# Attention and SwiGLU on one core: q and k columns dealt by groups of four heads, and all first-phase weights on one queue

## The chip, the cores and the metric

The kernel runs on one core of a Trainium2 chip. Such a core has a matrix engine (TensorE, PE in the profile, with PEld for its weight loads), a vector engine (DVE), a scalar engine (ACT), a general engine (POOL) and a synchronisation engine (SP) that here does nothing but issue DMAs. The metric is device time in microseconds; lower is better. Three runs of the kernel before took 590.81, 593.8 and 593.9 us, median 593.8.

## The reference

One token sequence x (2048 x 576, bf16) is normalised, and the result feeds two branches whose outputs are added to x.

```python
xn = layernorm(x)                                     # over 576, eps 1e-5
q, k, v = (xn @ wqkv) split into 32 heads of 18       # D = 576
scores = q @ k^T * 18**-0.5, causal, window 256
A = softmax(scores) @ v @ wo
B = (silu(xn @ w1) * (xn @ w3)) @ w2                  # F = 4608
out = x + A + B
```

## The kernel before

The sequence is worked off in four chunks of 512 tokens. Each chunk has three stages, one after the other on PE: QKV (about 13.6 us), the first phase (36 units of the first MLP product, w1 and w3, with the attention of the chunk dealt in between, 85 to 91 us), and the second phase (the product with w2 and the output product with wo, 42 to 46 us). Chunk 0 begins with the load and layernorm of the tokens instead of a ready xnT. The layernorm of chunk c+1 runs within the first phase of chunk c, on DVE, POOL and PE (`ln_stats`, `ln_apply`, `xn_turn`).

A unit u computes 128 of the 4608 hidden columns: 9 pairs of matmuls (line 646), each pair on the two halves of PE's rows, one into the bank of "up" and one into that of "gate"; then a tanh on ACT (654) and two operations on DVE (660, 663) that write hT. Its weights come in sets: `load_w13` fetches 512 columns of w3 and of w1 as two halves of 576 KB, enough for four units (`w13_at` names the buffer; there are three, and the fourth set of the run goes into a part of hT that is not needed yet). A set is released after unit 4m+3 and needed at unit 4m+12, so nine sets per chunk are on their way two or three ahead. Half w3 is issued by SP, half w1 by ACT, where `load_w13((), "act")` stands; in the first sets of the run SP issues both. One set per chunk is loaded in two halves during the second phase of the chunk before, at items 70 and 170 of its list.

The heads are 18 wide and so do not line up with 128 rows. QKV's matmuls for q and k give tiles of 128 columns, as the columns stand in wqkv: tiles 0 to 3 are q columns 0 to 511, 4 to 7 k columns 0 to 511, tile 8 the last 64 columns of both. They are evacuated into `stage`, one half of a pair by DVE, the other by ACT. From there `repack` moves every group of four heads by DMA into `qv` and `kv`, the layouts that the score matmuls want: a group needs 6 to 8 DMAs, more where it crosses a tile's border. `Groups` says which groups are complete after which tile. In chunks 1 to 3, groups 0 to 2 are issued during QKV, the other five at units 0, 1, 4, 7 and 8 (line 502 for all). `kv` has twelve blocks of keys: eight of the chunk, and the last four of the chunk before, which POOL copies (`keep_keys`).

Attention runs in steps: a score step is a few matmuls (541), an exponential on ACT into a slot (550: ten slots in `pt`, four in hT's tail, four in `stage` once it is free), masks on POOL (577). When two groups are done, `pv` multiplies with v, and after a normalisation DMAs pack the result into oT (631).

The order is written out in the program, engine by engine, by `add`; each engine works in that order, and an instruction that waits holds up all behind it. `_Prog.resolve` puts semaphore waits where data or buffers ask for them. Each of SP and ACT has a DMA queue of its own. On SP stand x tiles (296), w13 (316), w2 (333), the xnS swap (378), repack (502), oT (631) and the output (711). A counter of PE work (`clock`) decides between which matmul pairs of the units a score step is put.

## Time and profile before

The profiled execution took 591.38 us, 589.7 of it the span that the profile covers.

| stage | from to, us | length | PE busy | clock granted | GB/s |
|---|---|---|---|---|---|
| start and QKV, chunk 0 | 0 to 22.6 | 22.6 | 19.14 | 1.00 | 235 |
| first phase, chunk 0 | 22.6 to 109.3 | 86.7 | 82.64 | 0.98 | 175 |
| second phase, chunk 0 | 109.3 to 152.9 | 43.6 | 42.20 | 1.00 | 186 |
| QKV, chunk 1 | 152.9 to 166.5 | 13.6 | 13.60 | 1.00 | 55 |
| first phase, chunk 1 | 166.5 to 257.3 | 90.8 | 86.20 | 0.98 | 132 |
| second phase, chunk 1 | 257.3 to 301.7 | 44.4 | 42.17 | 1.00 | 169 |
| QKV, chunk 2 | 301.7 to 315.3 | 13.6 | 13.60 | 1.00 | 54 |
| first phase, chunk 2 | 315.3 to 400.9 | 85.6 | 84.09 | 1.00 | 140 |
| second phase, chunk 2 | 400.9 to 446.5 | 45.6 | 42.42 | 1.00 | 162 |
| QKV, chunk 3 | 446.5 to 460.0 | 13.5 | 13.50 | 1.00 | 55 |
| first phase, chunk 3 | 460.0 to 545.2 | 85.2 | 83.21 | 1.00 | 108 |
| second phase, chunk 3, to the end | 545.2 to 589.7 | 44.5 | 41.73 | 1.00 | 111 |

PE is the busiest engine at 96% of the span; DVE has 54%, ACT 43%, POOL 27%. The table is read row against row: the same work is done in the second phase of every chunk, and in the first phase of chunks 1 to 3 (but the last chunk has no next layernorm), so that differences between rows of one kind are waits or a slower clock. In the rows of the profile that follow, a group is line, engine, operation, output and inputs, shape and count; after the bar busy time and mean duration in ns, after the second bar the engine's idle time before these instructions and what ended it. A row of the timeline is start, length, what ran and how often, and in brackets the idle time before it. SPq and ACTq are the DMA issues of SP and ACT. "Issue" as a releaser means that the profile shows no wait that ended.

### The profile page before, as it was taken

Reading aid. Unit: us, or ns where it says so; the run is one execution under the profiler, and the core shown is the slowest. Engines: PE = TensorE matmul, PEld = TensorE weight load, DVE = VectorE, ACT = ScalarE, POOL = GpSimd, SP = SyncE. Lnnn points to the kernel's source line nnn. Section 1 sums busy time; section 2 is a strip of 40 time slices with the busy share of each in tenths; the row PEclk is TensorE's granted clock in tenths of the full one; section 3 lists DMA queues with packets and bytes.
Section 4 is the critical chain, followed back from the end, with each engine's and each line's share of the span. In section 5 each row is a group of like instructions: output and inputs, shape, how many; then the busy total and the mean of one; then the engine's idle time right before and its main releaser. Section 6 shows DMA issues by size and latency. Waiting matters only on the chain.

```text
span 589.7 us, 16005 instructions
## 1 busy us (share of the span) xinstructions
PE 564.5 (96%) x6885; PEld 359.9 (61%) x6885; DVE 316.2 (54%) x595; ACT 254.9 (43%) x350; POOL 161.4 (27%) x377
## 2 busy tenths in 40 slices
PE   7998999999999999899999999999899989999998
PEld 4443445677686454467768655457676875554776
DVE  6484887610377768651026777884103566777311
ACT  4354666300176667430017576771002766666000
POOL 6231443400032434240003244443000234434000
PEclk9998999999999999899999999999999999999999
DMA  8999689987317795767741768886773177851452
GB/s 248 179 178 182 129 165 224 204 197 186 95 26 145 123 203 111 155 134 192 173 107 29 138 121 176 148 182 150 166 179 80 39 135 145 159 100 51 114 153 67
DMA packets 119126, 83.87 MB, mean 142 GB/s; under 512 B 25552, under 2 KB 117904, under 8 KB 119056
## 3 DMA queue, kind: packets, MB, share of 16 engines
q1 hardware_dynamic: 98593, 63.41, 50.8%
q10 hardware_dynamic: 20463, 19.44, 16.5%
q8 instruction: 54, 0.88, 0.7%
q14 instruction: 16, 0.13, 0.1%
HBM read 71.29 MB, written 2.36 MB: 125 GB/s over the span
## 4 chain that ended last, share of the span: by engine, by line
PE 72%; DMA 13%; SPq 7%; issue 2%; DVE 2%; ACTq 2%; ACT 1%; POOL 0%
PE ps L646 39%; PE ps L696 14%; DMA w<-in_B_w_dram 9%; PE ps L410 8%; SPq L502 6%; PE ps L541 5%; PE ps L702 3%; PE ps L598 3%; ACTq L631 2%; DMA oT<-od 2%; DMA qv<-stage 1%; ACT xnT L372 0%; DMA xp<-in_A_x_dram 0%; PE ps L365 0%; DVE hT L663 0%
## 5 line engine op out<-in xcount | busy, mean ns | idle before, releaser
L646 PE MATMUL ps<-xnT,w 64*128 64x512 bf16 x1400 | 189.8, 378 | 5.3 <-issue 2.1
L646 PE MATMUL ps<-xnS,w 64*128 64x512 bf16 x1120 | 158.6, 377 | 2.0 <-issue 2.0
L696 PE MATMUL ps<-w,hT 128*128 128x288 bf16 x1152 | 148.6, 286 | 5.6 <-DMA w<-in_B_w_dram 5.4
L550 ACT ACTIVATE pt<-ps 128x1024 bf16<-128x1024 f32 (+1 forms) x112 | 113.2, 1010 | 75.2 <-PE ps L541 75.0
L660 DVE SCALAR_TENSOR_TENSOR gs<-th,ps 128x512 bf16<-128x512 bf16 x144 | 98.0, 680 | 84.9 <-ACT th L654 84.3
L696 PEld LDWEIGHTS ps<-w,hT 128*128 128x128 bf16 x1152 | 111.4, 98 | 38.1 <-DMA w<-in_B_w_dram 7.9
L646 PEld LDWEIGHTS ps<-xnT,w 64*128 64x128 bf16 x1400 | 78.6, 94 | 56.9 <-issue 6.3
L577 POOL TENSOR_TENSOR pt<-pt,mk 128x128 int32<-128x128 int32 (+1 forms) x199 | 80.1, 425 | 87.5 <-ACT pt L550 87.4
L663 DVE SCALAR_TENSOR_TENSOR hT<-gs,ps 128x512 bf16<-128x512 bf16 x144 | 98.9, 687 | 4.9
L654 ACT ACTIVATE th<-ps 128x512 bf16<-128x512 f32 x144 | 85.5, 593 | 27.2 <-PE ps L646 25.5
L646 PEld LDWEIGHTS ps<-xnS,w 64*128 64x128 bf16 x1120 | 65.0, 94 | 51.1 <-issue 2.9
L709 DVE TENSOR_TENSOR ofin<-ps,xp 128x288 bf16<-128x288 f32 x32 | 14.7, 458 | 128.5 <-PE ps L702 128.5
L422 ACT ACTIVATE stage<-ps 128x512 bf16<-128x512 f32 x16 | 9.6, 597 | 154.7 <-PE ps L410 149.5
L541 PE MATMUL ps<-qv,kv 64*128 64x320 bf16 (+2 forms) x720 | 64.4, 253 | 2.0 <-DMA qv<-stage 1.2
L541 PEld LDWEIGHTS ps<-qv,kv 64*128 64x128 bf16 x720 | 41.0, 94 | 32.7 <-issue 2.9
L577 POOL TENSOR_TENSOR hT<-hT,mk 128x128 int32<-128x128 int32 (+1 forms) x31 | 12.4, 422 | 171.4 <-ACT hT L550 171.4
L410 PE MATMUL ps<-xnT,wa 64*128 64x512 bf16 x288 | 34.3, 376 | 0.0
L550 ACT ACTIVATE stage<-ps 128x1024 bf16<-128x1024 f32 x24 | 24.6, 1024 | 13.7 <-PE ps L541 13.4
L620 DVE STREAM_TRANSPOSE od<-oq 128x256 bf16<-128x256 bf16 x64 | 25.8, 427 | 6.3 <-POOL oq L613 6.3
L702 PE MATMUL ps<-wo,oT 128*128 128x288 bf16 x160 | 24.8, 286 | 1.2 <-DMA oT<-od 1.2
L613 POOL TENSOR_TENSOR oq<-uq,rden 128x288 bf16<-128x288 f32 x16 | 10.8, 674 | 54.4 <-DVE rden L612 54.4
L410 PEld LDWEIGHTS ps<-xnT,wa 64*128 64x128 bf16 x288 | 16.7, 94 | 12.4 <-issue 0.7
(59 smaller groups left out, 337.0 us busy)
## 6 DMA issues: line engine op xcount, KB each, us to landing
w<-in_B_w_dram SPq DMA_DIRECT2D x41, 576.0 KB, 7.7
w<-in_B_w_dram SPq DMA_DIRECT2D x72, 288.0 KB, 3.6
w<-in_B_w_dram ACTq DMA_DIRECT2D x29, 576.0 KB, 7.1
xp<-in_A_x_dram SPq DMA_DIRECT2D x29, 144.0 KB, 8.3
out_dram<-ofin SPq DMA_DIRECT2D x32, 72.0 KB, 1.9
kv<-stage SPq DMA_DIRECT2D x105, 18.0 KB
oT<-od SPq DMA_DIRECT2D x84, 18.0 KB
qv<-stage SPq DMA_DIRECT2D x39, 36.0 KB
```

The costliest lines, as they stand in the source:

```text
L410: op = add("pe", lambda e, out_=out_, st=st, mv=mv, n=n, r0=r0, first=first: e.matmul(out_, st, mv, start=first, stop=(part == 1 and n == ...
L502: by, lambda e: e.dma_start(dst, src), r=reads, dma=f"{key[0]}_{g}", **kw)
L541: add("pe", lambda e, r0=r0, out_=out_, kb=kb, q0=q0, nb=nb: e.matmul(out_, kv[r0:r0 + 64, g, kb + NV - NB, :], qv[r0:r0 + 64, g, q0 * KB: ...
L550: add("act", lambda e: e.activation(pt_slot(sl)[:, 0:w, :], PS[:, SC[0]:SC[1] + 1, 0:w].rearrange("p r q -> p q r"), ACT.Exp, scale=scale) ...
L577: add("pool", lambda e, vb=vb, mm=mm: e.tensor_tensor(vb, vb, mm, ALU.mult), r=(key if n == 0 else []) + ["mk"], **{"w" if n == 0 else "j" ...
L620: add("dve", lambda e: e.transpose(od[i][:, c0:c0 + CH // 2], oq[:, c0:c0 + CH // 2]), r=["oq", "oq0"], **{"j" if half else "w": [("od", i)]})
L646: add("pe", lambda e, n=n, r0=r0, r=r, k=k, src=src: e.matmul(PS[:, b0 + r, :], wt[r0:r0 + 64, k, fl * 128:(fl + 1) * 128], src, start=(n ...
L654: add("act", lambda e: e.activation(th[i][:], PS[:, bg, :], ACT.Tanh, scale=0.5), r=[("ps", bg)], w=[("th", i)])
L660: add("dve", lambda e: e.scalar_tensor_tensor(out=gs[i][:], in0=th[i][:], scalar=1.0, in1=PS[:, bg, :], op0=ALU.add, op1=ALU.mult), r=[("t ...
L663: add("dve", lambda e: e.scalar_tensor_tensor(out=hT[:, u, :], in0=gs[i][:], scalar=0.5, in1=PS[:, bu, :], op0=ALU.mult, op1=ALU.mult), r= ...
L696: add("pe", lambda e: e.matmul(bank, hT[:, f, tt * 128:(tt + 1) * 128], w2[sl][:, k, :], start=(f == 0), stop=False), r=[("h", f), ("w2", ...
L702: add("pe", lambda e: e.matmul(bank, oT[:, k, tt * 128:(tt + 1) * 128], wo[:, k, d0:d0 + HD], start=False, stop=(k == 4)), r=[("oT", g) fo ...
```

## The change

There are five parts. In chunks 1 to 3 the columns of q and k are dealt anew: a tile t (0 to 7) holds the q columns of the four heads of group t (72), then the k columns of its first three heads (54), and two columns of the last head's k; tile 8 holds the k columns of the fourth head of groups 0 to 6, and two more of the last head. POOL builds these weights once, in chunk 0, with four copies into `wp`. Chunk 0 still uses the columns as they stand, now from a part of `pt`.

Since every group lies in one tile and in tile 8, one DMA can move the same rows of several groups: `repack_span` is called for group 0, for groups 1 and 2, and for groups 3 to 7 when all tiles are there. It replaces `repack` in chunks 1 to 3; units 0, 1, 4, 7 and 8 issue none any more. The slots in `stage` are all free from the start of the first phase.

All halves of w13 are issued by SP, none by ACT. The set that was loaded in the second phase is loaded in the QKV of the next chunk, behind the repack of groups 1 and 2. In chunk 0 the repack of group 0 comes ahead of set 1 and the two x tiles in SP's order, with its q DMAs on ACT; set 2 follows the repack of group 1. The keys of the chunk before move from the front of `kv` into a tensor of their own, `kb4`.

```diff
+        wv = sb("wv", [128, 5, D])
+        wp = sb("wp", [128, 5, 9, 128])
...
+        kv = sb("kv", [128, G, NB, 2 * KB])
+        kb4 = sb("kb4", [128, G, NV - NB, 2 * KB])
...
+        wa = pt[:, 0:6, :, :].rearrange("p n q r -> p (n q r)")[:, 0:10 * D].rearrange("p (k c) -> p k c", c=2 * D)
+        w8 = pt[:, 6, :, :].rearrange("p q r -> p (q r)")[:, 0:640].rearrange("p (k c) -> p k c", c=128)
+        wa_keys = ["wqk"] + [("pt", n) for n in range(6)]
...
+        def pair_of(c, i):
+            return (i, 4 + i) if c == 0 else ((8, 0), (1, 2), (3, 4), (5, 6))[i]
...
-        PROJ = [("q", 0), ("q", 1), ("v", 0), ("q", 2), ("v", 1), ("q", 3), ("v", 2), ("8", 8), ("v", 3)]
+        PROJ = [("q", 0), ("q", 1), ("v", 0), ("q", 2), ("v", 1), ("q", 3), ("v", 2), ("8", 7), ("v", 3)]
...
+        def keys_of(a, b, p0, n, p):
+            return kv[p0:p0 + n, a:b, :, KB * p:KB * p + KB].rearrange("q g b f -> q (g b) f")
+
+        def repack_span(a, b, eng, q_eng=None):
+            moves = []
+            gs_ = list(range(a, b))
+            for pr in range(2):
+                moves.append(("q", gs_, gs_, qv[64 * pr:64 * pr + 2 * Dh, a:b, :], stage[2 * Dh * pr:2 * Dh * (pr + 1), a:b, :]))
+            for i in range(3):
+                r0 = 4 * Dh + i * Dh
+                moves.append(("k", gs_, gs_, keys_of(a, b, 64 * (i // 2) + Dh * (i % 2), Dh, i % 2), stage[r0:r0 + Dh, a:b, :].rearrange("q g (b f) -> q (g b) f", f=KB)))
+            p0 = 64 + Dh
+            for g in gs_:
+                if g < G - 1:
+                    moves.append(("k", [g], [8], keys_of(g, g + 1, p0, Dh, 1),
+                                  stage[g * Dh:(g + 1) * Dh, 8, :].rearrange("q (b f) -> q b f", f=KB)))
+                else:
+                    for r in range(2):
+                        moves.append(("k", [g], range(9), kv[p0 + r:p0 + r + 2 * 9 - 1:2, g, :, KB:2 * KB], stage[126 + r:127 + r, :, :]))
+            seen = set()
+            for kind, gset, tset, dst, src in moves:
+                keys = [(kind, g) for g in gs_]
+                new = [k for k in keys if k not in seen]
+                old = [k for k in keys if k in seen]
+                seen |= set(keys)
+                add(q_eng if kind == "q" and q_eng else eng, lambda e, dst=dst, src=src: e.dma_start(dst, src),
+                    r=st_keys(*tset), w=new, j=old, dma=f"{kind}_{a}")
...
         xn_swap(0, ("sp", "sp"))
-        load_w13()
-        for t in (TB, TB + 1):
-            xslot[t] = load_x(t)
         proj_begin(0, ("v", TB - 1))
...
+        for n, (dst, src) in enumerate((
+                (wp[:, :, 0:G, 0:4 * Dh].bitcast(dt.float32), wq_),
+                (wp[:, :, 0:G, 4 * Dh:7 * Dh].bitcast(dt.float32), wk_[:, :, :, 0:3 * Dh].bitcast(dt.float32)),
+                (wp[:, :, 8, 0:7 * Dh].rearrange("p k (g c) -> p k g c", c=Dh), wk_[:, :, 0:G - 1, 3 * Dh:4 * Dh]),
+                (wp[:, :, :, 126:128], last))):
+            add("pool", lambda e, dst=dst, src=src: e.tensor_copy(dst, src), r=wa_keys, **{"j" if n else "w": ["wp"]})
...
         def issue_first(c, g):
             if g < 2:
-                repack(c, g, "sp")
+                repack(c, g, "sp", "sp" if g else "act")
+                load_w13()
+                if g == 0:
+                    for t in (TB, TB + 1):
+                        xslot[t] = load_x(t)
...
-        load_w13()
         repack(0, held.pop(0), "sp")
...
             if c:
-                free += [("sh", 0), ("sh", 2)]
+                free += [("sh", n) for n in range(4)]
...
                     if got:
-                        for g in groups.got(got):
-                            if g < 3:
-                                repack(c, g, "sp", "sp" if g else "act")
-                            else:
-                                turned.append(g)
+                        if got == ("q", 0):
+                            repack_span(0, 1, "sp", "act")
+                        elif got == ("q", 1):
+                            repack_span(1, 3, "sp")
+                            load_w13()
+                        elif got[0] == "8":
+                            repack_span(3, G, "sp")
...
-                if u in ((0, 1, 4, 7, 8) if c else ()):
-                    repack(c, turned.pop(0), "sp")
...
-                    load_w13((), "act")
+                    load_w13()
...
-                if n in (70, 170):
-                    load_w13_half()
```

## The prediction

> **What bounds the kernel now.** First the page: which engine is full, and where. Then the stretches by stage, then PE's timeline wherever PE was idle, then the queue that PE was waiting for.
>
> ```profile
> PE 564.5 (96%) x6885; PEld 359.9 (61%) x6885; DVE 316.2 (54%) x595; ACT 254.9 (43%) x350; POOL 161.4 (27%) x377
> ...
> L696 PE MATMUL ps<-w,hT 128*128 128x288 bf16 x1152 | 148.6, 286 | 5.6 <-DMA w<-in_B_w_dram 5.4
> ```
>
> PE is busy 564.5 of 589.7 us, and the change leaves its matmuls as they are: the same number, sizes and order. So nothing but the 25.2 us in which PE idles, and the time it runs slowed, can be won. The next lines are PE's timeline at its stalls; the bracket is the idle time before the row.
>
> ```profile
> 28.32 0.40 PE L541 MATMUL ps<-qv,kv 64*128 64x320 bf16 x4 [1.19 <-DMA qv<-stage]
> 52.33 1.89 PE L646 MATMUL ps<-xnT,hT 64*128 64x512 bf16 x8 [2.79 <-issue]
> 184.79 0.39 PE L646 MATMUL ps<-xnT,w 64*128 64x512 bf16 x2 [0.77 <-DVE hT L663]
> 206.02 0.82 PE L646 MATMUL ps<-xnT,w 64*128 64x512 bf16 x6 [1.29 <-DMA w<-in_B_w_dram]
> 245.21 0.39 PE L646 MATMUL ps<-xnT,w 64*128 64x512 bf16 x1 [2.13 <-issue]
> 289.29 2.99 PE L696 MATMUL ps<-w,hT 128*128 128x288 bf16 x23 [1.41 <-DMA w<-in_B_w_dram]
> 419.83 0.67 PE L696 MATMUL ps<-w,hT 128*128 128x288 bf16 x4 [1.35 <-DMA w<-in_B_w_dram]
> 434.04 1.16 PE L696 MATMUL ps<-w,hT 128*128 128x288 bf16 x8 [1.24 <-DMA w<-in_B_w_dram]
> 486.93 0.80 PE L646 MATMUL ps<-xnS,w 64*128 64x512 bf16 x5 [1.99 <-issue]
> ```
>
> Most of these are late DMAs. Two queues show why: in chunk 0, w13 set 3 (into hT) is issued at 35.85 and lands at 52.24, while ACT has sent half of set 4, needed four units later, ahead of it at 32.44; in the second phase, a w13 half on SP stands in front of five w2 tiles.
>
> ```profile
> 35.85 1.34 SPq L316 DMA_DIRECT2D hT<-in_B_w_dram  x2
> ...
> 281.84 0.63 SPq L316 DMA_DIRECT2D w<-in_B_w_dram  x1
> 282.51 9.31 SPq L333 DMA_DIRECT2D w<-in_B_w_dram  x5
> ```
> ```profile
> 32.44 0.74 ACTq L316 DMA_DIRECT2D w<-in_B_w_dram  x1
> ```
>
> A stall can cost more than its length. These stretches hold the 2.79 and the 2.13 us stall:
>
> ```profile
> 49.00:56.00 7.00, 4.21 (x32) 1.71 (x28) 2.20 (x4) 1.70 (x3) 0.46 (x1) 0.76 1.11 175
> 243.00:250.00 7.00, 4.87 (x35) 2.36 (x36) 3.98 (x9) 2.52 (x4) 1.82 (x4) 0.76 0.31 76
> ```
>
> The granted clock (third number from the end) falls to 0.76, a loss of 7 x 0.24 = 1.7 us each, of which I take 1.5 for the first (part of it fell on idle time). No other stall has this; the one of 1.99 us has not.
>
> **The change, part by part.** The profiled execution took 591.38 us; the median of the three runs is 593.8 (590.81, 593.8, 593.9), 2.4 above.
>
> *The w13 halves out of the second phase.* Items 70 and 170 no longer send 576 KB through SP in front of w2. Stalls behind such a half: chunk 0, 0.21 (127.13) and 0.57 (139.95); chunk 1, 1.41 and, for oT packs crossing it, 0.79 (275.16); chunk 2, 0.20, 1.35, 0.39 and 1.24. Sum 6.2 us. The last chunk's second phase has no such half and no stall, which is the control; 0.6 us in chunk 0 lies behind the xnS swap and stays. Taken: -6.1.
>
> The set goes into the next chunk's QKV, behind the two small repacks: SP starts repacking 4.0 us into it (156.86), 11 issues of 0.79 end near 166, so the set is issued there, and it lands within 8.6 us (a set issued on SP alone at 29.32 landed at 37.96). Unit 8 needs it at 184.8, 10 us later. Cost 0; without that cover, what comes late is unit 8.
>
> *Repack.* Chunks 1 to 3 issue 56 repack DMAs each, 54 on SP (42.5 us of it, median 0.79), until 203.10 in chunk 1. The new dealing needs 6 + 7 + 11 = 24, 22 on SP: 17.4 us, 25 us less per chunk. PE waits on this queue at 206.02: 1.29 us for a w13 half that SP issued only at 196.62, though ACT's came at 196.13; that goes (-1.3). The x tile of unit 0 was issued at 178.40, DVE waited 2.69 us for it, and PE behind DVE 0.77 + 0.41 in chunk 1 and 0.98 + 0.41 in chunk 2. Now 4 + 7 + 2 + 11 = 24 issues precede it in place of 26, 2 us earlier at best, but behind a w13 set in the same queue. Between 0 and -2.6 I take half, -1.3. The larger span for groups 3 to 7 is hidden: the first of its score steps is the 16th.
>
> *Chunk 0's order.* Group 0 no longer waits behind set 1 and two x tiles: its data now leaves at 17.87 with little in front, so the 1.19 us stall goes (-1.2). Two q DMAs go to ACT (0.76 each) between evacuations that have 1.34 us of gap: at most 0.2 us late, 0. Set 1 waits for the four k DMAs: issued near 21.1 instead of 13.97, landed near 29.7 by the 8.6 us above; unit 4 starts at 32.2, 31.0 without the stall. Slack 1.3, cost 0; at the 13 us that this set needs now it would be 3.1 late. Set 2 keeps its place; set 3 is issued about 0.8 us later, but without ACT's halves in front: some 45 to 47 against 48.4. Stall and slow clock go, -4.3.
>
> Next late would be set 4 or 5: its second half now leaves with the first (47 instead of 32.44). 47.4 + 8.6 = 56.0 against a need of 58.3; set 5, 57 + 8.6 = 65.6 against 66.8. SP's issues in this stretch sometimes take 3.2 us instead of 0.8 (37.30, 47.54). Bounds 0 and +4.3 (a stall like that of set 3); nearer to the slack than to the stall, taken +1.0.
>
> *All w13 halves on SP.* 29 issues (18.6 us) leave ACT and cost SP as much over the whole run, less than the repack frees. ACT's idle time before tanh was mostly PE's (25.5 of 27.2 us), so nothing on PE's path goes: 0. A set then needs SP for both halves, but SP's half was the late one already.
>
> *POOL's four copies into the dealt weights.* By the copy of 256 f32 in 402 ns: 1440 + 1080 f32, then 630 + 90 bf16 elements, 2.3 + 1.7 + 1.0 + 0.1 = 5.1 us. POOL is idle from 19.20 for 10.65 us, until the first mask. 0; uncovered, masks would be late, with 20 units until their PV. The attention slots that now hold q and k weights are first written by the fifth exponential, near 40. 0.
>
> Sum: -6.1 - 1.3 - 1.3 - 1.2 - 4.3 + 1.0 = -13.2, so 578.2. Two of three runs lay 2.4 higher than the profiled one; I add a third of that: **579**.
>
> The Trainium skill's "TensorE: Matmul & The Clock Gate" (What's actually happening) has the clock halved after an idle window of about 3.4 us. Here stalls of 2.79 and 2.13 us were followed by it, so the trace decides. By the page the stall at 49.54 would be worth 2.8, and the sum -11.7.
>
> **The rivals.**
>
> *The "issue" stalls go too.* At 243.08 and 484.93 PE stopped in the middle of a unit whose data it had been reading. A queue moves 54 packets (0.88 MB) of instructions; with 13,770 PE instructions that is one packet per 255. Packets usually start about 10 us apart; before these stalls the distances were 16.0 us (226.71 to 242.70) and 15.3 us (468.99 to 484.24): PE ran out of instructions. Both times w13 halves were in flight on two queues (234.22 and 234.23; 476.67 and 477.66). With one queue the packet may get through: 2.13 + 1.7 + 1.99 = -5.8, about 573. Against: the same bytes are in flight, and four x tiles with the first. The rule for such a gain is in the skill's "DMA: Bandwidth & Descriptors" (Queues, rings and completion order): each DMA engine takes turns between the queues that have work. No row here shows the turns.
>
> *Chunk 0 gains nothing.* Set 1, 4 or 5 is late in place of set 3, and costs a stall and a slow clock again: 5.5 of the sum is lost and up to 3 us more added: 584 to 588.
>
> *The stalls only move* (the set in QKV is late for unit 8, x tiles are late as ever): 589 to 595.
>
> *Slower: sets late throughout on one queue.* A set has 8 units of 2.16 = 17.3 us from release to use. Behind SP's longest wait for oT (7.3 us) and nine oT issues of 0.72, two halves land 7.3 + 6.5 + 0.7 + 8.6 = 23 us after release: 5.8 late, with the clock 7.5. Two such sets eat the gain up (15 of 13.2 us), so the third decides; three, one in each later chunk, make +22 on 578: 600. Against: SP's half has had all of this in front of it already, and made PE wait once, 1.29 us.
>
> **How the numbers follow.** Forecast (575 to 583) 0.46; issue stalls gone too 0.14; chunk 0 gains nothing 0.20; stalls only move 0.08; slower 0.12. Half a per cent of 593.8 is 3 us, about what a measurement of this kernel can tell: faster means under 590.8 (0.80), same 0.08, slower over 596.8 (0.12). The range goes from the second case's lower side, 571, to 592, halfway into the fourth; it leaves out the slower case and the ends of two others, under 2 in 10.
>
> **What would show it.** The second phase of chunks 0 to 2 near 42 us without stalls on w; SP's last repack issue in chunk 1 before 180 instead of at 203; no stall near 49 and 0.98 or more of the clock there; no stall at the first score. Wrong, if PE waits for w at units 4, 16 or 20 of chunk 0, at unit 8 of later chunks, or at several unit fours in a row.

## The result, and the profile after

The changed kernel takes 587.18 us in the median of 20 runs (582.34 to 592.84), the kernel before 591.87 us in 20 runs: a ratio of 0.9918, 95% interval 0.9889 to 0.9947. It is 0.8% faster, where 2.5% was forecast: 4.7 us out of 13 to 15. Ratios here leave out executions over 1.5% above their kernel's fastest, among them the one that was profiled with the result, so that a ratio need not equal that of two medians. The profile read here is the changed kernel's second (f0_after below: 588.08 us, span 586.4; the kernel before had 591.38 and 589.7). It is called "the changed kernel" below, the other one "its first profile".

The page of the changed kernel: engines, and the groups of the two large loops.

```profile
PE 565.0 (96%) x6885; PEld 347.1 (59%) x6885; DVE 315.9 (54%) x595; ACT 255.0 (43%) x350; POOL 164.6 (28%) x381
...
L686 PE MATMUL ps<-xnT,w 64*128 64x512 bf16 x1400 | 190.0, 380 | 7.2 <-DVE hT L703 4.6
...
L736 PE MATMUL ps<-w,hT 128*128 128x288 bf16 x1152 | 147.3, 286 | 0.4 <-DMA w<-in_B_w_dram 0.4
```

PE's work is the same to the instruction. The idle time ahead of L736, the second phase's matmuls, has gone from 5.6 to 0.4 us, and the idle time ahead of L686, those of the first phase, has grown from 5.3 to 7.2; 5.0 us stand newly ahead of L638, the PV matmuls. So the gain was made where it was forecast, and part of it was given back elsewhere. PE's timeline at its stalls shows where (start, length, row; the bracket is the idle time before it):

```profile
114.03 1.15 PE L736 MATMUL ps<-w,hT 128*128 128x288 bf16 x8 [0.36 <-DMA w<-in_B_w_dram]
180.03 0.39 PE L686 MATMUL ps<-xnT,w 64*128 64x512 bf16 x2 [2.54 <-DVE hT L703]
212.24 0.28 PE L638 MATMUL ps<-stage,va 64*20 64x256 bf16 x3 [2.32 <-issue]
242.65 0.37 PE L686 MATMUL ps<-xnT,w 64*128 64x512 bf16 x1 [1.70 <-issue]
327.73 0.39 PE L686 MATMUL ps<-xnT,w 64*128 64x512 bf16 x2 [2.07 <-DVE hT L703]
338.61 0.20 PE L638 MATMUL ps<-hT,va 64*20 64x64 bf16 x2 [2.70 <-issue]
482.15 0.60 PE L686 MATMUL ps<-xnS,w 64*128 64x512 bf16 x3 [2.23 <-issue]
```

The only wait for a w13 set that is left is one of 0.48 us at unit 4 of chunk 0 (31.32). Two waits for DVE stand at the start of chunks 1 and 2, where 0.77 and 0.98 us stood; four "issue" stalls, where PE stops in the middle of work whose data it has, stand in place of two. The stretches by stage, and then around the issue stalls (length, PE, PEld, DVE, ACT, POOL busy, granted clock, DMA share, GB/s):

```profile
22.50:104.60 82.10, 81.13 (x1053) 41.74 (x1048) 64.04 (x120) 49.45 (x68) 30.14 (x73) 1.00 0.98 191
104.60:146.50 41.90, 41.54 (x404) 32.58 (x404) 8.26 (x18) 0.60 (x1) 3.24 (x8) 1.00 0.70 170
160.10:252.90 92.80, 85.93 (x1164) 45.12 (x1158) 64.31 (x120) 59.15 (x76) 35.82 (x87) 0.98 0.72 140
252.90:294.60 41.70, 41.70 (x426) 33.00 (x424) 8.40 (x19) 0.60 (x1) 3.42 (x9) 1.00 0.57 152
308.20:399.70 91.50, 86.00 (x1165) 46.32 (x1162) 64.30 (x121) 59.22 (x76) 35.95 (x87) 0.98 0.71 140
399.70:441.40 41.70, 41.70 (x428) 33.00 (x428) 8.36 (x18) 0.60 (x1) 3.34 (x8) 1.00 0.61 155
455.00:541.90 86.90, 84.67 (x1125) 44.50 (x1120) 57.04 (x97) 57.42 (x76) 32.27 (x76) 0.98 0.60 118
...
209.00:216.00 7.00, 4.68 (x115) 2.44 (x96) 3.50 (x7) 1.33 (x2) 1.50 (x3) 0.81 0.97 189
240.00:247.00 7.00, 5.30 (x59) 2.97 (x57) 4.80 (x10) 4.23 (x6) 2.59 (x7) 1.00 0.36 100
335.00:342.00 7.00, 4.30 (x118) 2.32 (x118) 2.88 (x6) 1.62 (x2) 1.85 (x5) 0.83 0.38 67
479.00:486.00 7.00, 4.76 (x35) 1.84 (x31) 3.11 (x7) 1.98 (x3) 2.36 (x5) 0.79 0.68 120
```

The second phases of chunks 1 and 2 take 41.70 us and PE is busy in all of it; chunk 0's first phase has no stall of note and the full clock. Three of the four issue stalls are followed by a slowed clock, 3.4 us at half speed or 1.7 us each; the kernel before had one such window in chunks 1 to 3. With the same borders in both kernels the sum is:

| stage | before | changed | difference | forecast |
|---|---|---|---|---|
| chunk 0, first phase | 86.6 | 82.1 | -4.5 | -4.5 |
| second phases and the QKV behind them, chunks 0 to 2 | 57.3, 58.1, 59.2 | 55.5, 55.3, 55.3 | -8.5 | -6.1 |
| first phases of chunks 1 to 3 | 90.7, 85.6, 85.1 | 92.9, 91.4, 86.9 | +9.8 | -2.6 |

The rest (start and last chunk's end) gives -0.2: together -3.4, with rounding the difference of the spans (3.3 us). The first two rows gave what the whole forecast amounted to, 13 us. The third took most of it back, and 9.6 of its 9.8 us come apart as x tile 5.24 instead of 2.57 us (+2.7), the stall on w at 206.02 gone (-1.3), issue stalls 8.95 instead of 4.12 us (+4.8) and two more half-clock windows (+3.4). These are single executions: in its first profile the changed kernel has 7.7 us of issue stalls.

### The profile page after: what moved, and what is told of

The parts are those of the page before. It is cut to its first block, busy times and chain, and to the rows that moved or that the text cites. A ratio compares the mean times of both kernels' runs of the same rounds, so it can differ in the third digit from the quotient of the medians.

```text
span 589.9 us, 15893 instructions
## 1 busy us (share of the span) xinstructions
PE 566.6 (96%) x6885; PEld 347.5 (59%) x6885; DVE 315.5 (53%) x595; ACT 255.1 (43%) x350; POOL 164.6 (28%) x381
## 4 chain that ended last, share of the span: by engine, by line
PE 83%; SPq 6%; DVE 5%; DMA 4%; issue 2%; ACT 0%; POOL 0%
PE ps L686 38%; PE ps L736 24%; PE ps L420 9%; PE ps L581 5%; SPq L541 4%; PE ps L742 3%; PE ps L638 3%; DMA xp<-in_A_x_dram 3%; DMA w<-in_B_w_dram 1%; DVE hT L703 1%; DVE gs L700 1%; SPq L513 1%; DVE xn L358 1%; SPq L321 1%; PE ps L370 0%
## 5 line engine op out<-in xcount | busy, mean ns | idle before, releaser
L686 PE MATMUL ps<-xnT,w 64*128 64x512 bf16 x1400 | 188.6, 378 | 6.6 <-DVE hT L703 4.9
L686 PE MATMUL ps<-xnS,w 64*128 64x512 bf16 x1120 | 158.1, 378 | 2.3 <-issue 2.3
L736 PE MATMUL ps<-w,hT 128*128 128x288 bf16 x1152 | 150.4, 290 | 4.6 <-DMA w<-in_B_w_dram 4.5
L736 PEld LDWEIGHTS ps<-w,hT 128*128 128x128 bf16 x1152 | 113.3, 99 | 36.9 <-DMA w<-in_B_w_dram 4.8
L686 PEld LDWEIGHTS ps<-xnT,w 64*128 64x128 bf16 x1400 | 71.9, 94 | 62.3 <-issue 6.3
L686 PEld LDWEIGHTS ps<-xnS,w 64*128 64x128 bf16 x1120 | 59.6, 94 | 59.0 <-issue 6.5
L581 PE MATMUL ps<-qv,kv 64*128 64x320 bf16 (+4 forms) x528 | 56.5, 261 | 0.6 <-DVE xnT L377 0.6
L581 PEld LDWEIGHTS ps<-qv,kv 64*128 64x128 bf16 x528 | 28.9, 94 | 26.3 <-DVE xnT L377 1.8
L420 PE MATMUL ps<-xnT,wp 64*128 64x512 bf16 (+1 forms) x270 | 29.5, 355 | 0.0
L420 PE MATMUL ps<-wv,xnT 64*128 64x288 bf16 x288 | 22.5, 290 | 0.6 <-ACT xnT L377 0.4
```

What stands on the lines that cost most here:

```text
L420: op = add("pe", lambda e, out_=out_, st=st, mv=mv, n=n, r0=r0, first=first: e.matmul(out_, st, mv, start=first, stop=(part == 1 and n == ...
L581: add("pe", lambda e, r0=r0, out_=out_, kb=kb, q0=q0, nb=nb: e.matmul(out_, kb4[r0:r0 + 64, g, kb + NV - NB, :] if kb < 0 else kv[r0:r0 + ...
L686: add("pe", lambda e, n=n, r0=r0, r=r, k=k, src=src: e.matmul(PS[:, b0 + r, :], wt[r0:r0 + 64, k, fl * 128:(fl + 1) * 128], src, start=(n ...
L736: add("pe", lambda e: e.matmul(bank, hT[:, f, tt * 128:(tt + 1) * 128], w2[sl][:, k, :], start=(f == 0), stop=False), r=[("h", f), ("w2", ...
```

## The experiments

The theory put to the test: the gain of the second phase is made by moving the third set; the same set, put into the QKV ahead of the repack of groups 3 to 7, holds back the x tile behind it in SP's queue; and the issue stalls are PE running out of instructions, worse with the denser traffic of one queue. The rivals: the halves' move from ACT to SP is what costs, the place of the instructions in the program sets the issue stalls and the traffic has no part in them, or the new dealing is not needed.

### The x tile

SP's queue in the changed kernel at the start of chunk 1 (issue time, length, row):

```profile
155.42 4.16 SPq L541 DMA_DIRECT2D kv<-stage  x5
159.62 1.35 SPq L321 DMA_DIRECT2D w<-in_B_w_dram  x2
161.01 1.67 SPq L541 DMA_DIRECT2D qv<-stage  x2
162.73 12.64 SPq L541 DMA_DIRECT2D kv<-stage  x9
175.41 0.47 SPq L301 DMA_DIRECT2D xp<-in_A_x_dram  x1
```

Five repack issues ahead of the set take 4.16 us, 0.83 each; the nine behind it take 12.64, 1.40 each. Three of the nine are slow: the second and third of the three 90-KB DMAs that move groups 3 to 7 at once (2.15 and 4.12 us) and the one behind them (1.25); the set is on its way until 169.70. It takes both, as two kernels that follow show. In e2, which has no set there, the same nine take 8.69 us, and these three 1.43, 1.34 and 0.79:

```profile
167.11 8.69 SPq L541 DMA_DIRECT2D kv<-stage  x9
```

In e7, which has the set but the small repack DMAs of the old dealing (18 KB for k), the eight behind it take 0.6 to 0.9 us each (168.66 to 175.10; its second half landed at 175.62).

The x tile is issued 25.1 us after SP's first repack of this chunk (150.33); in the kernel before it was 21.5 (156.86 to 178.40), although two more issues stood ahead of it there.

**e1_x_first** sends the x tile in the QKV, ahead of the set:

```diff
                             repack_span(1, 3, "sp")
+                            if c + 1 < NC:
+                                xslot[(c + 1) * TB + 1] = load_x((c + 1) * TB + 1)
                             load_w13()
...
-                loads = {0: () if c == 0 else (1,), 8: (2,), 17: (3,)}
+                loads = {8: (2,), 17: (3,)}
```

> The changed kernel, with one x tile per chunk moved: in chunks 1 and 2 the second x tile of the next chunk is issued in QKV right behind the repack of groups 1 and 2, ahead of the w13 set and of the span of groups 3 to 7, instead of at unit 0 behind them. Theory 1 (the tile is held up on SP by the full queue, DVE waits for it and PE waits behind DVE): the stalls of 2.42 + 0.32 us in chunk 1 and 1.84 + 0.31 us in chunk 2 are gone, first phases of both chunks 2 to 3 us shorter, the whole 4 to 6 us below the changed kernel (587.2), about 582. Rival (what took the gain back is the stalls called issue, from the instruction packets): under 1 us better than the changed kernel, the stalls behind DVE replaced by others.

Measured: 580.52 us in the median of 6, the kernel before 594.06 on that chip; ratio 0.9806 [0.9754, 0.9857]. SP's queue and PE's timeline in chunk 1:

```profile
160.52 0.48 SPq L301 DMA_DIRECT2D xp<-in_A_x_dram  x1
161.05 1.36 SPq L321 DMA_DIRECT2D w<-in_B_w_dram  x2
162.45 1.67 SPq L541 DMA_DIRECT2D qv<-stage  x2
164.16 11.91 SPq L541 DMA_DIRECT2D kv<-stage  x9
```
```profile
192.43 0.82 PE L686 MATMUL ps<-xnT,w 64*128 64x512 bf16 x5 [1.02 <-issue]
211.39 0.28 PE L638 MATMUL ps<-stage,va 64*20 64x256 bf16 x3 [2.49 <-issue]
240.31 0.37 PE L686 MATMUL ps<-xnT,w 64*128 64x512 bf16 x1 [1.88 <-issue]
```

The nine issues behind the set are as slow as before, but the tile is ahead of them. The DVE stalls of chunks 1 and 2 are gone, and the issue stalls stay. That the set in front of the tile was the cause has three witnesses more below (e2, e5, and e1's second run).

**e1b_x_first**, the same kernel again, and **f0_after**, the changed kernel unedited, on one other chip:

> The kernel with the x tile first once more, beside the changed one: 5 to 9 us faster than it (theory 1), no stall of PE behind DVE in chunks 1 and 2. Rival: within 2 us of it.

> The changed kernel once more, unedited, on the same chip as the next three, so that they can be set against it and not against the kernel before alone. If the waits behind the x tile are its own (theory 1), its profile shows them again near 186 and 334 us, 1.8 us or more each, and its runs lie 5 to 9 us above the kernel with the x tile first. If the first comparison was between chips, the two lie within 2 us.

Measured: 583.34 us (6 runs), 0.9886 [0.9838, 0.9934], against 587.64 us (12 runs), 0.9959 [0.9931, 0.9987], for the changed kernel. The order of the tile is worth 4.3 us here, a little under what was expected; chunks 1 and 2 have no DVE stall again.

**e8_before_x**: the kernel before with this one edit.

```diff
                                         turned.append(g)
+                        if got == ("q", 1) and c + 1 < NC:
+                            xslot[(c + 1) * TB + 1] = load_x((c + 1) * TB + 1)
...
-                loads = {0: () if c == 0 else (1,), 8: (2,), 17: (3,)}
+                loads = {8: (2,), 17: (3,)}
```

> The kernel before, with one thing alone: the second x tile of chunks 1 and 2's next chunk issued in QKV ahead of group 1's repack's successors instead of at unit 0. By the profile of before it removes 0.77 + 0.41 and 0.98 + 0.41 us of PE's idle time: 2 to 3 us faster than before, ratio about 0.995. Rival (the x tile is where the whole difference between the changed kernel and the one with the x tile first lies, and would be had without the change): 5 us or more faster than before, ratio 0.99 or less.

Measured: 587.45 us (12 runs) against 591.57, but 1.0006 [0.9968, 1.0044] by the ratio. The medians of all runs are 4.1 us apart and the ratio shows nothing, so whether the early tile gains by itself is open. The DVE stalls at the starts of chunks 1 and 2 are gone, another of 1.29 us stands in chunk 2 (356.48), and the stalls of the second phase stay (58.1 and 58.9 us to the end of the next QKV in chunks 1 and 2). By either measure the early x tile alone doesn't make up e1, which is 6.5 and 13.5 us below the kernel before by the medians, 1.1 and 1.9% by the ratio.

### The third set, the queue of the halves, the dealing

**e2_set_back** puts the third set back where it was:

```diff
                             repack_span(1, 3, "sp")
-                            load_w13()
...
                 p2_item(c, item, xs)
+                if n in (70, 170):
+                    load_w13_half()
```

> The changed kernel, with the third set of w13 back in two halves at items 70 and 170 of the second phase, SP alone as issuer. Theory 1 (the halves in front of w2 made the second-phase stalls): second phases of chunks 1 and 2 go from 41.7 back to 44 to 45 us, +5 to +6 in all; the x tile comes earlier in QKV, -2 to -3; net +2 to +4 against the changed kernel, about 590. Rival (the second phase got better through the shorter SP queue, not through the set): second phases stay near 42, and the time falls by 2 to 3.

Measured: 588.77 us (12 runs), 0.9941 [0.9897, 0.9984]. Second phase and QKV take 58.3 and 60.4 us in chunks 1 and 2, against 55.3 each. PE's timeline:

```profile
274.73 0.66 PE L736 MATMUL ps<-w,hT 128*128 128x288 bf16 x4 [0.66 <-DMA w<-in_B_w_dram]
289.10 8.51 PE L736 MATMUL ps<-w,hT 128*128 128x288 bf16 x68 [1.53 <-DMA w<-in_B_w_dram]
418.17 0.67 PE L736 MATMUL ps<-w,hT 128*128 128x288 bf16 x4 [1.33 <-DMA w<-in_B_w_dram]
419.54 1.11 PE L742 MATMUL ps<-wo,oT 128*128 128x288 bf16 x5 [0.70 <-DMA oT<-od]
434.00 8.50 PE L736 MATMUL ps<-w,hT 128*128 128x288 bf16 x68 [0.86 <-DMA w<-in_B_w_dram]
```

These are the stalls of the kernel before, at the same places; and with no set in front of the x tile the DVE stall is gone from chunks 1 and 2. So the set's move wins 3.0 and 5.1 us in the second phases of chunks 1 and 2 (up to the end of the next QKV) and loses 5.2 of it at the x tile; the intervals of the two kernels overlap.

**e3_act_halves** gives the units' second halves back to ACT:

```diff
                 if u % 4 == 3 and u < NF - 4 and (c or u != 15):
-                    load_w13()
+                    load_w13((), "act")
```

> The changed kernel, with the second half of each set of the units (not of the first sets, nor of the one in QKV) issued by ACT again. Theory 1 (one queue or two changes the order only): in chunk 0 the stall before unit 12 is back, 2 to 3 us and the slow clock, and the wait for w2 in its second phase shrinks by as much; chunks 1 to 3 within 1 us; in all within 2 us of the changed kernel. Rival (all halves on one queue hold up PE's instruction packets): the stalls called issue fall from 7.7 us in all to about 4, and the kernel is 3 to 5 us faster than the changed one.

Measured: 594.25 us (12 runs), 1.0018 [0.9981, 1.0054]: 0.6 to 1% slower than the changed kernel, which neither side expected. Most of it lies in chunk 0, whose first phase takes 90.2 us instead of 82.1. PE's timeline, then SP's and ACT's queues:

```profile
43.20 1.04 PE L686 MATMUL ps<-xnT,w 64*128 64x512 bf16 x8 [2.65 <-issue]
55.59 1.88 PE L686 MATMUL ps<-xnT,hT 64*128 64x512 bf16 x8 [3.69 <-issue]
```
```profile
36.97 4.77 SPq L321 DMA_DIRECT2D hT<-in_B_w_dram  x2
...
40.58 0.68 ACTq L321 DMA_DIRECT2D w<-in_B_w_dram  x1
```

Set 3, issued at 36.97 and 37.67, landed at 49.38 and 55.49, 0.1 us before PE goes on; ACT had sent half of set 4 at 31.01, as in the kernel before, and its half of set 5, needed eight units after set 3 and issued 2.9 us behind it, landed at 54.91, ahead of it. In the changed kernel set 3 was issued at 36.76 and 37.53 and landed at 45.06 and 47.07. That is the mechanism by which the prediction took the stall of 52.33 away, shown by putting it back.

**e7_old_deal** is the reverse: the kernel before with every part of the change but the dealing and its spans.

```diff
         xn_swap(0, ("sp", "sp"))
-        load_w13()
-        for t in (TB, TB + 1):
-            xslot[t] = load_x(t)
...
-                repack(c, g, "sp")
+                repack(c, g, "sp", "sp" if g else "act")
+                load_w13()
+                if g == 0:
+                    for t in (TB, TB + 1):
+                        xslot[t] = load_x(t)
...
+                        if got == ("q", 1):
+                            load_w13()
...
-                    load_w13((), "act")
+                    load_w13()
...
-                if n in (70, 170):
-                    load_w13_half()
```

> The kernel before with all of the change but the new dealing of columns: chunk 0's new order on SP, all w13 halves on SP, the third set in QKV behind the repack of group 2; repack still in 56 DMAs per chunk. If the dealing is worth something by the SP time that it frees (25 us per chunk), sets and the x tile are later than in the changed kernel: stalls of PE on w13 near units 12 and 16 of chunks 1 to 3 and longer ones behind DVE, 594 to 600 us. Rival (SP's time is hidden, and the order of the weights is all): within 2 us of the changed kernel's 587.

Measured: 591.16 us (12 runs), 1.0068 [1.0024, 1.0112]. PE's timeline at unit fours of chunks 1 to 3:

```profile
202.75 0.82 PE L646 MATMUL ps<-xnT,w 64*128 64x512 bf16 x6 [1.58 <-issue]
348.12 1.47 PE L646 MATMUL ps<-xnT,w 64*128 64x512 bf16 x6 [2.96 <-issue]
498.21 1.89 PE L646 MATMUL ps<-xnT,w 64*128 64x512 bf16 x8 [4.45 <-issue]
```

The profile names no releaser here, but the sets that these rows read landed at 202.66 and 498.12, 0.1 us before PE goes on: these are late sets, behind the long repack on the one queue. With 32 repack issues more per chunk the other parts together are 0.7% slower than the kernel before by the ratio (0.4 us faster by the medians of all runs); with the dealing, 0.4 to 0.8% faster. The time lies between the two expectations. A set late in each later chunk (9.0 us of stalls together) is what the prediction's slower rival priced, though behind the repack and not behind oT, and in these profiles the dealing is what keeps it away.

### What is left in chunk 0

The changed kernel's first profile had a wait for w2 in chunk 0 (4.50 us, at 120.09), with 6.8 us at half clock behind it; in the second profile it was 0.36 us. The load of wo was suspected. **e4_wo_early** sends wo eleven units earlier (`if c == 0 and u == 14:` in place of 25).

> The changed kernel, with the load of wo (0.65 MB) in chunk 0 issued at unit 14 instead of 25. Theory 1 (chunk 0's saving turned into a wait for w2 at 115.6 because the DMA engines are full from 80 to 117 us): with 0.65 MB less in that stretch, 3 to 4 us at its 170 to 200 GB/s, the 4.50 us stall falls to 1 us or less and the slow clock behind it goes: 4 to 7 us below the profiled run of the changed kernel, 3 to 5 on the median. Rival (w2 is late because its issue stands on SP behind oT and xnS): the stall stays at 4 us or more.

Measured: 590.55 us (12 runs), 0.9941 [0.9893, 0.9989]. The stall on w2 is gone (second phase and QKV of chunk 0: 55.0 us), but DVE stalls of 1.27, 3.23 and 1.97 us and issue stalls of 9.1 us stand in its place: no gain. Nor is wo the whole cause, since f2 below, with wo as early, has the stall again.

**f1_x_all_wo** adds e4's edit to e1, and sends every chunk's third x tile a unit earlier (`loads = {7: (2,), 17: (3,)}`). **f2_spaced** is f1 with the second half of each set sent two units after the first:

```diff
                 if u % 4 == 3 and u < NF - 4 and (c or u != 15):
-                    load_w13()
+                    load_w13_half()
+                if u % 4 == 1 and u > 4 and (c or u != 17):
+                    load_w13_half()
```

> As the one before, and two more loads moved in the same sense: the third x tile of every chunk at unit 7, ahead of the set released there, instead of at unit 8 behind it, and wo at unit 14 of chunk 0 instead of 25. Theory: in chunk 0 PE's wait behind DVE near 66 us (0.6 to 2.6 us in the profiles so far) and the wait for w2 near 115 us (0.8 to 4.5) are gone, 2 to 4 us below the kernel with one x tile first, clock 0.997 or better. Rival (what is moved ahead only makes a w13 set late): PE waits at units 16 or 20 of chunk 0 instead, and the time is the same within 1.5 us.

> As the one before, with the second half of each set issued two units (4.3 us) after the first, instead of right behind it. Theory A (an instruction packet is late behind queued w13 descriptors, 1.2 MB at a time): with 0.6 MB at a time the stalls called issue in chunks 1 to 3 fall to half of those of the kernel before it in count and length, 2 to 4 us faster. Rival (what counts is the bytes in all, not how many stand in the queue at once): the stalls are as many and as long, and the time is within 1.5 us.

Measured, on the chip of e1b: 582.56 us, 0.9883 [0.9838, 0.9927], and 583.18 us, 0.9842 [0.9787, 0.9897] (6 runs each); e1b 583.34. In f1 chunk 0's stalls are gone, in f2 one on w2 is back (3.86 us at 115.86), issue stalls are 7.7 and 6.2 us, so halves sent apart didn't bring them down to half. None of this can be told from e1b: the last microseconds of chunk 0 are below what the runs resolve.

### The issue stalls

Every issue stall of chunks 1 to 3, but for e7's three late sets, ends shortly after a packet of the queue that the page calls "instruction" (16 KB each, 54 in every kernel; one packet takes about 1.2 us). In the changed kernel:

| stall | last packet ended | PE goes on after | packet before that started |
|---|---|---|---|
| 209.91 to 212.24 | 210.68 | 1.56 us | 11.0 us earlier |
| 240.96 to 242.65 | 241.22 | 1.43 us | 15.2 us earlier |
| 335.91 to 338.61 | 337.33 | 1.28 us | 19.1 us earlier |
| 479.91 to 482.15 | 480.50 | 1.65 us | 13.9 us earlier |

In all kernels with such stalls it is 1.25 to 1.7 us. Counting shows it more sharply: 13,770 matmuls and weight loads in 54 packets are about 256 a packet, and if PE's work is counted from its start, PE goes on with number 192 to 195 of a block of 256 after every one of the 67 such stalls of the 20 profiles, in shifted kernels as in the others. So PE stops where a packet ends and waits for its instructions, as the prediction read it. Two executions of one kernel stall at the same points of the program: e1 at 191.40, 208.90, 238.43, 354.35 and 470.63, e1b, which runs 4 to 10 us later there, at 195.65, 215.82, 246.56, 364.23 and 480.48. Is it the traffic, or the place?

**e5_no_w13** leaves out the w13 loads from the fourth set of chunk 1 on, 28 MB of transfers, and computes with what lies in the buffers.

```diff
+            if k >= NFC + 3:
+                return
             add(eng, lambda e: e.dma_start(
```

> The changed kernel without the w13 loads of chunks 1 to 3 (from the fourth set of chunk 1 on): the units there multiply with whatever the buffers hold, and some 27 MB less is moved, so the output is not the reference's. It asks what the stalls called issue, which end 1.3 to 1.6 us after an instruction packet, come from. Theory A (the packet is late because w13 fills the DMA engines): in chunks 1 to 3 none of them is left, and about 6 us go with them. Theory B (the packet is asked for too late at fixed places of PE's program, whatever the DMAs do): at least three of them remain in chunks 1 to 3, in about the same units (second or third PV of chunk 1, near unit 28 of chunk 1, near unit 10 of chunk 3), 1 to 2.5 us each. Under both the waits behind the x tile are gone or small, as no set stands in front of it; second phases as before.

Measured: 574.17 us (2 runs), 0.9794 [0.9703, 0.9884]. Chunks 1 to 3 have no issue stall at all. As g3 below has none either with all its traffic, the starts of all packets of these chunks say more. In every kernel the earliest start when PE has reached about number 160 of a block, some 290 instructions ahead of the border where PE would stop. From that place to the packet's start e5 takes 1.2 us in the mean, the other nineteen 2.0 to 3.1 us. So the packets come earlier without that traffic, and the stalls go with it. The x tile shows as well: chunk 1, which still has a set in front of it, has its DVE stall (3.38 us), and chunk 2, which has none, has not.

**e6_shift** (e1), **g2_before_20**, **g1_before_40**, **g3_before_80** (the kernel before) and **h3_x_80** (e1) leave the traffic alone and put 20, 60 or 140 PE instructions more into the program's start, by splitting the ten matmuls that warm PE up into more and narrower ones of the same total width:

```diff
-        warm(4, 10)
+        warm(4, 40, 128)
```

**h1_x_act** and **h2_x_act_40** are e1 with e3's halves on ACT, without and with 60 instructions more.

> The kernel with the x tile first (580.5), and the ten warming matmuls of 512 columns at the start replaced by forty of 128: the same columns, 30 more matmuls and 30 more weight loads, so that all of PE's later program stands 60 instructions further along against the packets of about 255. Theory B (places in the program): the stalls called issue move or vanish, at least three of the five of that kernel's profile are in other units or gone, and their sum changes by over 2 us in either direction. Theory A (DMA traffic at that time): they stay in the same units, with about 8 us in all, and the time is within 1.5 us of 580.5.

> The kernel before, its ten warming matmuls of 512 columns replaced by forty of 128: 30 matmuls and 30 weight loads more at the start, nothing else changed, so only the place of PE's instructions within the packets of about 255 moves. The profile of before had two stalls called issue behind a packet in chunks 1 to 3 (2.13 and 1.99 us), those of the changed kernel and its variants three to seven. If the number depends on where the packets' borders fall (theory B): it changes to three or more here too, without any of the change, and the time rises by 3 to 8 us. If it was the change's traffic that made the further ones (theory A): two or fewer, in the same units, time within 2 us of before.

> The same with twenty of 256 columns, 20 instructions on. Theory B: another number or other units than in before and than with forty, 0 to 6 of them. Theory A: two or fewer, in the same units as before.

> The same with eighty of 64 columns, 140 instructions on, more than half a packet. Theory B: another number again, three or more in at least one of the three kernels of this kind. Theory A: two or fewer in all three.

> The kernel with the x tile first, the second halves of the units' sets issued by ACT again. Counted are the stalls behind instruction packets in chunks 1 to 3 (after 130 us, over 0.6 us, ended 1.2 to 1.75 us after a packet): 5 each in the two profiles with all halves on SP, 9.3 and 9.0 us. If one queue makes them (its 1.2 MB stand in a row): 3 or fewer, under 5.5 us, as in the kernel with ACT's halves and the late x tile (3, 5.1 us). If not: 4 or more, over 7 us. Chunk 0's stall near unit 12 comes back under both, 3 to 5 us with its slow clock.

> The same with PE's program shifted by 60 instructions, to be set against the shifted kernel with all halves on SP (7 stalls, 13.3 us). If one queue makes them: 4 or fewer, under 8 us. If not: 5 or more, over 9 us.

> The kernel with the x tile first and all halves on SP, PE's program shifted by 140 instructions. The kernel before with this shift had no such stall in chunks 1 to 3. If the place in the program alone decides: none or one here, under 2 us. If the change's traffic adds its own: 3 or more, over 5 us.

Measured: issue stalls over 0.6 us that end behind a packet, in chunks 1 to 3 of the one profiled execution of each, with the time of the kernel and its ratio to the kernel before on the same chip:

| kernel | instructions added | halves on | stalls | their sum, us | median, us | ratio |
|---|---|---|---|---|---|---|
| before | 0 | SP and ACT | 2 | 4.1 | | |
| g2_before_20 | 20 | SP and ACT | 3 | 4.1 | 590.35 (10 runs) | 1.0027 [0.9984, 1.0070] |
| g1_before_40 | 60 | SP and ACT | 3 | 8.6 | 591.37 (10) | 1.0044 [1.0000, 1.0088] |
| g3_before_80 | 140 | SP and ACT | 0 | 0 | 598.11 (4) | none |
| e8_before_x | 0 | SP and ACT | 1 | 1.9 | 587.45 (12) | 1.0006 [0.9968, 1.0044] |
| e3_act_halves | 0 | SP and ACT | 3 | 5.1 | 594.25 (12) | 1.0018 [0.9981, 1.0054] |
| h1_x_act | 0 | SP and ACT | 4 | 5.5 | 579.16 (2) | 0.9815 [0.9606, 1.0023] |
| h2_x_act_40 | 60 | SP and ACT | 3 | 8.5 | 587.00 (8) | 0.9936 [0.9885, 0.9986] |
| e7_old_deal | 0 | SP | 2 | 4.7 | 591.16 (12) | 1.0068 [1.0024, 1.0112] |
| e2_set_back | 0 | SP | 3 | 5.2 | 588.77 (12) | 0.9941 [0.9897, 0.9984] |
| changed | 0 | SP | 4 | 8.9 | 587.64 (12) | 0.9959 [0.9931, 0.9987] |
| its first profile | 0 | SP | 5 | 7.7 | 587.18 (20) | 0.9918 [0.9889, 0.9947] |
| e4_wo_early | 0 | SP | 4 | 9.1 | 590.55 (12) | 0.9941 [0.9893, 0.9989] |
| e1_x_first | 0 | SP | 5 | 9.3 | 580.52 (6) | 0.9806 [0.9754, 0.9857] |
| e1b_x_first | 0 | SP | 5 | 9.0 | 583.34 (6) | 0.9886 [0.9838, 0.9934] |
| f1_x_all_wo | 0 | SP | 5 | 7.7 | 582.56 (6) | 0.9883 [0.9838, 0.9927] |
| f2_spaced | 0 | SP | 4 | 6.2 | 583.18 (6) | 0.9842 [0.9787, 0.9897] |
| e6_shift | 60 | SP | 7 | 13.4 | 585.16 (12) | 0.9948 [0.9900, 0.9997] |
| h3_x_80 | 140 | SP | 4 | 12.9 | 586.20 (2) | none |

On the chip of e6, e7 and e8 the ratio of the medians of all runs is 0.6 to 0.8% lower than the ratio given.

The place matters: 60 instructions that change nothing else take the kernel before from 4.1 to 8.6 us and e1 from 9.3 to 13.4. The times don't follow these sums: g1 has 4.4 us more of them than the kernel before in its profile, and 0.5 us more time in the median (0.4% by the ratio), where 3 to 8 us were expected. The rest seems to matter too: e1 with its halves on one queue has more than with ACT's at both shifts where the two can be compared (9.0 to 9.3 against 5.5, and 13.4 against 8.5), and the kernel before less at 140 (0 against 12.9). That points to one queue, at 4 to 5 us. It isn't settled: each entry is one execution, e2 and e7 have their halves on one queue and only 5.2 and 4.7, h1 and h2 fell between the marks set for them, h2's ratio can't be told from e6's, and nothing in the trace shows when PE asked for a packet, so that a late request and a late answer look alike. g3's time says nothing: its profiled execution took 583.85 us, the other three 597.80 to 602.44, and why isn't known.

## Why the prediction was right and wrong

*The w13 halves out of the second phase (-6.1)* was right: chunks 1 and 2 lost 2.8 and 3.9 us, 6.7 together, to the 41.7 us that PE needs, and e2 brought the stalls back. Chunk 0 gained 1.8 in the profile read here; it varies, from 55.0 to 63.2 us over the kernels, with the wait for w2, which the prediction didn't have. The set's new place cost no wait at unit 8, as forecast.

*Chunk 0's first phase (-1.2 - 4.3 + 1.0 = -4.5)* was right: -4.5 in the profile, and -4.3 in the first one; that it is right to the tenth is luck, since the +1.0 for a late set 4 or 5 stood for a stall that didn't come, and the 0.48 at unit 4 was priced at 0. No stall at the first score, none near 49, the clock at 1.00, and units 8, 16 and 20 didn't wait for w. Unit 4 did, for 0.48 us: set 1 landed at 31.23, not near 29.7, and the slack of 1.3 us was used up. Its rival, that set 1, 4 or 5 is late in place of set 3, didn't occur; e3 shows what set 3 loses by ACT's halves. "ACT to SP, 0" held only because its gain had been counted under set 3: with the halves back on ACT this stage takes 8.1 us more.

*POOL's copies (0)* were right: no stall waits for POOL. None waits for *the spans* either, but they were not free: the prediction priced the 22 issues on SP at the 0.79 us of the old small ones, 17.4 us, and in chunk 1 they took 23.4 us, nearly all of the difference in the nine behind the set.

*The w13 half behind the repack at 206.02 (-1.3)* was right: no unit of later chunks waits for w.

*The x tile, "between 0 and -2.6 I take half, -1.3"* is the first step that failed, and its sign: it came to +2.7. The bounds reached from "nothing gained" to "all gained" and left out a loss, although the same paragraph put a w13 set in front of the tile in the same queue. The row that should have priced it stood two paragraphs on: SP's issues take 3.2 us instead of 0.8 while sets are in flight. It names two such issues in chunk 0; two behind this set would have been 2 x 2.4 = 4.8 us, and it was 5.2 (12.64 less nine of 0.83), 4.0 of it by the set (12.64 against e2's 8.69) and the rest by the spans' size. SP's last repack in chunk 1 was forecast before 180; it ended at 175.4, and at 184.0 in the first profile, in both 15 us after unit 0 began.

*The issue stalls* are the second step. The forecast left them as they were; a rival at 0.14 let them go, by a rule of the Trainium skill's "DMA: Bandwidth & Descriptors" (Queues, rings and completion order), that each DMA engine takes turns between the queues with work. The runs went the other way: +4.8 us, and +3.4 of clock behind them. By that rule fewer queues should help PE's packets; in the pairs of the table above the kernels with one queue have more, though that isn't settled, and no run shows the turns. The reading as missing instructions was right, the sign wasn't, and "the same bytes are in flight" was no ground for leaving the term at zero when every shift of the traffic or of the program moves it between 0 and 13 us. Why the changed kernel has more than the kernel before stays open: the kernel before, shifted by 60 instructions, has as much (8.6 us).

*The clock.* The prediction priced a half-clock window only at two stalls, and let the trace decide between it and the skill's "TensorE: Matmul & The Clock Gate" (What's actually happening), which wants an idle window of about 3.4 us. Here no length divides them: the stalls of 2.32, 2.70 and 2.23 us were followed by 1.7 us of loss each, e1b's of 2.02, 2.02 and 1.99 too, while e1's of 2.49 and 3.11 us were not. The place on a grid of time does. In each trace the granted clock changes only at whole multiples of 3.413 us, counted from its first change, and on this grid it is the share of PE's busy time in one window that tells whether the next window runs at half speed. The first three rows are the changed kernel around its stall of 2.32 us, the others e1 around that of 3.11 us (PE's busy time stands behind the length, the granted clock third from the end):

```profile
206.53:209.95 3.42, 3.38 (x119) 1.92 (x114) 2.38 (x6) 1.99 (x3) 0.77 (x3) 1.00 1.03 185
209.95:213.37 3.42, 1.13 (x21) 0.61 (x22) 1.88 (x4) 0.46 (x1) 0.00 (x0) 1.00 0.97 199
213.37:216.78 3.41, 3.41 (x24) 1.39 (x22) 0.67 (x2) 1.21 (x2) 1.50 (x3) 0.50 0.83 152
...
468.93:472.35 3.42, 1.71 (x19) 0.62 (x15) 2.45 (x5) 1.02 (x1) 0.86 (x3) 1.00 1.13 205
472.35:475.76 3.41, 2.01 (x24) 1.11 (x26) 0.00 (x0) 1.15 (x2) 0.69 (x3) 1.00 0.84 150
475.76:479.17 3.41, 3.41 (x40) 1.86 (x38) 2.95 (x7) 2.11 (x4) 1.53 (x4) 1.00 0.22 28
```

The shorter stall lies in one window and leaves PE busy for 1.13 us of it; the longer one is shared by two, each still busy for half its time or more. In the 19 profiles that hold changes of the clock (e8's holds none), from 20 us on, 37 of 37 windows with under 40% busy were followed by half speed, 8 of 11 with 40 to 43%, and 0 of 3,080 with more. So a stall costs 1.7 us more when it takes about 2 us out of one window, and for stalls of 2 to 4 us it is luck where the grid lies: e1's profile, with 9.3 us of issue stalls and a clock of 1.00, had it. What is lost this way differs from run to run: (1 - clock) x time is 4.1 us in the mean of the changed kernel's 12 runs, 2.6 in the kernel before's 17 on the same chip and 8.7 in e3's 12, and within the first 20 runs of the changed kernel it goes with the time (correlation of clock and time -0.78).

*The slower rival* (sets late on one queue) didn't occur, for the reason given against it; e7 shows its price without the dealing, behind the repack, with stalls of 1.58, 2.96 and 4.45 us at one set in each later chunk. *The stalls only move*, at 0.08 and meant for the set at unit 8 and the x tiles, is nearest to what happened, though the stalls that it meant to stay in the second phase went and others came. The measured 587 to 588 lies in the range, 8 to 9 us above the forecast. In the profile it is 9.8 (-3.4 against -13.2): 4.0 at the x tile and 8.2 in issue stalls and clock, less 2.4 that the second phases gave beyond their term.

## What to carry to other kernels

A transfer that is moved into a queue is paid for by what stands behind it there: price it with the queue's own slowest rows, and let the late work behind it (here the x tile, 4 us for two moved lines) go first. When stalls are removed and PE is the bound, ask which stalls depend on the traffic and on the place in the program, since these change with any edit; give such a term bounds on both sides instead of zero. A schedule that wins can be worth nothing (e7) without the part that makes room for it in the queue.

The best kernel of the study is e1: 580.52 and 583.34 us on two chips, 1.1 to 1.9% faster than the kernel before; f1 and f2 can't be told from it, and h1 has two runs. Its halves on SP in chunk 0 and on ACT later, which the table would suggest, wasn't tried.

## What the runs showed of the hardware

- PE stops for 0.6 to 4.0 us, up to seven times in chunks 1 to 3, until 1.25 to 1.7 us after a 16-KB instruction packet ends. It always stops at the same place of a packet, number 192 to 195 of 256 instructions. Traffic makes the packets late (1.2 us in the mean with 28 MB left out, 2.0 to 3.1 else), and 60 extra instructions at the start, which move the borders, made 3 to 5 us more of these stalls.
- The Trainium skill's "Runtime: NRT & Kernel Launch" (Instruction fetch mechanics) calls the cost of such a border mostly hidden. Of the 54 packets here that holds for all but none to seven; seven cost 13.4 us of 587, and half-clock windows can follow.
- SP's DMA issues take 0.8 us each. Behind a w13 set in flight single large ones take 2 to 4 us (2.15 and 4.12 for 90 KB, 1.43 and 1.34 without the set), small ones 0.6 to 0.9 (e7): nine in 12.64 us behind a set, 8.69 without it.
- The granted clock changes on a grid of 3.413 us. A window with PE busy under 40% is followed by one at half speed (37 of 37), one with over 43% never (0 of 3,080).
